# Attention with the keys on the partitions: scores written transposed, values standing still, no row maximum

## The chip, the cores and the metric

The kernel runs on one core of a Trainium2 chip. The metric is device time in microseconds, as the median of runs of the whole kernel; a profile is taken of one execution. TensorE does matrix products into PSUM, VectorE and ScalarE read PSUM and SBUF, GpSimd reads SBUF alone, and SP, ScalarE and GpSimd issue the DMAs.

## What is computed

Eight batches of twelve heads, 448 tokens of 64 dims each, all float32. The rows of q and k are divided by their root mean square and multiplied by a gain; attention follows; the heads are put side by side to 768 channels; then a gate picks 128 of the 448 tokens of each batch, and a feed-forward part is added to those alone.

```python
q_n, k_n = (rmsnorm(q, g_q), rmsnorm(k, g_k))        # x / sqrt(mean(x*x) + 1e-06) * g
scores = 1/sqrt(64) * q_n @ k_n^T
scores = scores - np.max(scores, axis=-1, keepdims=True)
attn = np.exp(scores)
attn = attn / (np.sum(attn, axis=-1, keepdims=True) + 1e-09)
x = attn @ v                                          # (B,H,S,D) -> (B, S, H*D)
...
scores = np.einsum('bsd,d->bs', x, w_gate)
top_idx = np.argpartition(-scores[b], capacity)[:capacity]   # capacity = 128
h = np.maximum(x[b, top_idx] @ w1, 0.0)               # 768 -> 1024
out[b, top_idx] = x[b, top_idx] + sigmoid(scores[b, top_idx])[:, None] * (h @ w2)
```

## The kernel before

Token 4p + j of a batch lies on partition p (112 of them), at place j. Heads come in 24 groups of four; a group is loaded by three DMAs from SP (`load`, L72), three groups ahead, and normalized by `normalize` (L131): GpSimd squares q and k (L138), VectorE sums (L139), GpSimd takes the power -0.5 (L144) and multiplies (L152). `transpose_pair` (L162) brings q and k of two heads onto 128 partitions through TensorE and PSUM, and multiplies by the gains.

The work then runs in 192 units, a unit being 112 queries of two heads. `scores` (L187) makes two matmuls, one per head, whose operands lie on partitions 0 to 63 and 64 to 127, with 112 queries on the output's partitions and 448 keys along the free dimension; VectorE takes the negative row maximum of both heads (L201), and ScalarE the exponential with that bias and the row sum (L206). `transpose_probs` (L216) turns the probabilities by eight TensorE transposes (L222), which VectorE (L229) and ScalarE (L231) copy to SBUF. `values` (L237) makes eight matmuls (each two passes in float32), with the turned probabilities standing still and 64 columns of v moving (L245); VectorE divides by the row sum into x (L253 to L255).

`mixture` (L265) is the feed-forward part of a batch, written as a generator of 16 pieces, one of which is issued after each unit of the next batch: gate scores, ranks and picks on VectorE, the gather (L368), both products (L400, L420) on TensorE, evacuations on ScalarE and VectorE, and an indirect DMA that adds into the output. The last batch's part has no units beside it.

The main loop (L446) issues at step i the scores of unit i, the transposes of unit i-1 and the values of unit i-2. A scheduler orders each engine's queue before the run; the semaphores follow from the data.

Of the kernel before, what the change touches and what calls it, by code (L numbers as in the profile page):

```python
# [17 lines left out]
def _bcast_row(ap_1d: bass.AP, parts: int) -> bass.AP:  # L18
    return dataclasses.replace(ap_1d, ap=[[0, parts]] + [list(x) for x in ap_1d.ap])


@with_exitstack
def kernel(
    ctx: ExitStack,
    tc: tile.TileContext,
    q: bass.AP,
# [7 lines left out]
    moe_capacity: int,  # L34
    out: bass.AP,
):
    """Token 4 p + j of a batch lies on partition p, at place j, everywhere on the chip."""
    nc = tc.nc

    B, H, S, D = q.shape  # L40
    CP = 112
# [28 lines left out]
    loaded = {}  # L70

    def load(n):  # L72
        """The n-th group of heads."""
        b, h0 = n // NG, n % NG * GH
        for nm, src in (("q", q), ("k", k), ("v", v)):
            t = load_pool.tile(
                [CP, GH, NJ, D], F32, tag=nm, name=nm, bufs=5 if nm == "v" else 3
            )
            nc.sync.dma_start(
                out=t.rearrange("p h j d -> p h (j d)"),  # L80
                in_=src[b, h0 : h0 + GH].rearrange("h (p j) d -> p h (j d)", j=NJ),
            )
            loaded[nm, n] = t
# [13 lines left out]
                out=t[D * half : D * (half + 1), :], in_=g.rearrange("(d one) -> d one", one=1)  # L97
            )

    # Which tokens (j', p') of a batch come before token (p, j).  # L100
    before = const.tile([CP, NJ, NJ, CP], F32, name="before")
    nc.vector.memset(before, 1.0)
    for j in range(NJ):
# [25 lines left out]
        nc.sync.dma_start(out=w2, in_=moe_w2.rearrange("(c p) f -> p c f", p=128))  # L129

    def normalize(n):  # L131
        """Rows of q and k of a group of heads over their rms, heads innermost."""
        ss = norm_pool.tile([CP, 2, GH, NJ], F32, name="ss")
        rinv = norm_pool.tile([CP, 2, GH, NJ], F32, name="rinv")
        for i, nm in enumerate("qk"):
            t = loaded[nm, n]
            sq = norm_pool.tile([CP, GH, NJ, D], F32, name="sq")
            nc.gpsimd.tensor_tensor(out=sq, in0=t, in1=t, op=OP.mult)  # L138
            nc.vector.tensor_reduce(out=ss[:, i], in_=sq, axis=AX.X, op=OP.add)  # L139
        nc.gpsimd.tensor_scalar(  # L140
            out=ss, in0=ss, scalar1=1.0 / D, scalar2=1e-6, op0=OP.mult, op1=OP.add
        )
        flat = "p i h j -> p (i h j)"
        nc.gpsimd.tensor_tensor(  # L144
            out=rinv.rearrange(flat),
            in0=ss.rearrange(flat),
            in1=neg_half.to_broadcast([CP, 2 * GH * NJ]),
            op=OP.pow,
        )
        for i, nm in enumerate("qk"):  # L150
            t = norm_pool.tile([CP, NJ, GH, D], F32, tag=nm + "n", name=nm + "n")
            nc.gpsimd.tensor_tensor(  # L152
                out=t.rearrange("p j h d -> p h j d"),
                in0=loaded.pop((nm, n)),
                in1=rinv[:, i, :, :, None].to_broadcast([CP, GH, NJ, D]),
                op=OP.mult,
            )
            loaded[nm + "n", n] = t
# [1 line left out]
    pairs = {}  # L160

    def transpose_pair(b, c):  # L162
        """q and k of two heads with their dims on the partitions, times g (and the scale)."""
        n, h = b * NG + 2 * c // GH, 2 * c % GH
        qT = tr_pool.tile([128, S], F32, name="qT")
        kT = tr_pool.tile([128, S], F32, name="kT")
        for nm, dst in (("q", qT), ("k", kT)):
            ps = ps_tr.tile([128, NJ, CP], F32, tag="tr", name="qk_ps")
            for j in range(NJ):
                nc.tensor.transpose(  # L170
                    out=ps[:, j, :],
                    in_=loaded[nm + "n", n][:, j, h : h + 2, :].rearrange("p h d -> p (h d)"),
                    identity=ident[:CP, :CP],
                )
            ps = ps.rearrange("p j r -> p (j r)")
            if nm == "q":
                nc.vector.tensor_scalar(
                    out=dst, in0=ps, scalar1=gq2, scalar2=scale, op0=OP.mult, op1=OP.mult
                )
            else:  # L180
                nc.scalar.activation(out=dst, in_=ps, func=AF.Copy, scale=gk2)  # L181
        pairs[b, c] = qT, kT
# [80 lines left out]
        return ps_moe.tile([128, 512], F32, tag="moe", name="moe_ps")  # L263

    def mixture(b):  # L265
        """The feed-forward part of batch b, in pieces."""
        x = xs.pop(b)
        nc.sync.dma_start(
            out=out[b].rearrange("(p j) c -> p (j c)", j=NJ), in_=x.rearrange("p j c -> p (j c)")
# [18 lines left out]
        nc.vector.tensor_copy(out=spread, in_=sc[:, :, None].to_broadcast([CP, NJ, CP]))  # L288
        yield

        # The scores of all tokens on every partition, then each token's rank: how many
        # tokens have a higher score, or the same and come before it.
        row_ps = bank()
        for j in range(NJ):
            nc.tensor.transpose(
# [29 lines left out]
        rank = moe_pool.tile([CP, NJ], F32, name="rank")  # L325
        nc.vector.tensor_add(out=rank, in0=higher, in1=equal)

        # Per token: its gate, and its row of the output.
        extra = moe_pool.tile([CP, NJ, 2], F32, name="extra")
        # sigmoid(s) = exp(min(s, 0)) / (exp(min(s, 0)) + exp(-max(s, 0))) has no overflow.  # L330
        parts = moe_pool.tile([CP, 2, NJ], F32, name="parts")
        nc.vector.tensor_scalar_min(out=parts[:, 0], in0=sc, scalar1=0.0)
        nc.vector.tensor_scalar(
# [5 lines left out]
        nc.vector.tensor_mul(out=extra[:, :, 0], in0=parts[:, 0], in1=parts[:, 1])  # L339
        nc.vector.tensor_scalar_add(out=extra[:, :, 1], in0=token_f, scalar1=float(b * S))  # L340
        if CAP % 128:
            # The last slots hold tokens past the capacity: they get nothing added.
            kept = moe_pool.tile([CP, NJ], F32, name="kept")
            nc.vector.tensor_scalar(
                out=kept, in0=rank, scalar1=float(CAP), scalar2=None, op0=OP.is_lt
# [150 lines left out]
```

## Time and profile before

| | us |
|---|---|
| median of 3 runs (1129.56 to 1142.35) | 1139.58 |
| span of the profiled execution | 1137.9 |
| TensorE busy in it | 1009.8 |
| VectorE, ScalarE, GpSimd busy | 619.0, 396.2, 335.3 |
| mean granted clock of TensorE | 0.903 of full speed |

Busy times are unions over an engine's instructions; those of TensorE are modelled at their ends, so that the distance from one start to the next tells more than a duration. PE is the matmul, PEld the weight load that precedes it; a float32 matmul stands as two of each. The granted clock is 1.0 (2.4 GHz) or 0.5 (1.2 GHz) at each moment, and a stretch's figure is a mean over it. The idle time that a row shows is that just before the instruction, with what ended it.

### The profile page before, as it was taken

The numbers are of one execution on the slowest core, as the hardware profiler recorded it, in microseconds if no ns is written. First come the engines' busy times: TensorE is split into PE (matmuls) and PEld (weight loads), VectorE is DVE, ScalarE is ACT, GpSimd is POOL, SyncE is SP. The second block draws the span as 40 slices with busy tenths as digits, with TensorE's granted clock in tenths as the row PEclk, the third lists the DMA queues.
The fourth block names the chain that finished last, engine by engine and source line by source line (L and its number), as shares of the span: only waits on it lengthen the run. The fifth ranks groups of instructions, "written<-read, shape, count | busy, mean of one in ns | idle before, by whom it ended". The sixth has DMA issues, their size and how long they took to land.

```text
span 1137.9 us, 17977 instructions
## 1 busy us (share of the span) xinstructions
PE 1009.8 (89%) x7264; PEld 795.4 (70%) x7264; DVE 619.0 (54%) x1379; ACT 396.2 (35%) x1049; POOL 335.3 (29%) x165
## 2 busy tenths in 40 slices
PE   0598988997989988999889998899898999999966
PEld 0476776875877666886668767687576877787764
DVE  3455577445764357644575446845567447943640
ACT  0232444232533334333343333333343334532400
POOL 7926314405314054041342231440513301100000
PEclk9675888998989979899789997899988999999979
DMA  6901203103201022021231030310302001100110
GB/s 173 334 2 49 49 1 98 50 1 63 78 21 50 1 63 98 1 49 18 46 98 28 22 63 1 97 50 1 63 13 86 17 1 15 50 1 1 15 49 14
DMA packets 37938, 54.98 MB, mean 48 GB/s; under 512 B 1776, under 2 KB 34032, under 8 KB 36960
## 3 DMA queue, kind: packets, MB, share of 16 engines
q1 hardware_dynamic: 36384, 50.68, 15.6%
q0 software_dynamic: 1152, 3.15, 1.9%
q8 instruction: 58, 0.95, 0.3%
q14 instruction: 24, 0.20, 0.1%
q10 hardware_dynamic: 320, 0.00, 0.0%
HBM read 39.67 MB, written 14.16 MB: 47 GB/s over the span
## 4 chain that ended last, share of the span: by engine, by line
PE 67%; POOL 21%; DVE 5%; issue 4%; DMA 1%; ACT 1%; POOLq 0%; SPq 0%; ACTq 0%
PE av L245 23%; PE sc L193 13%; PE pt_ps L222 13%; POOL rinv L144 10%; PE moe_ps L420 6%; PE moe_ps L400 4%; POOL sq L138 4%; PE qk_ps L170 4%; PE moe_ps L368 3%; POOL qn L152 3%; POOL kn L152 3%; DVE ss L139 2%; DVE nmax L201 2%; DMA q<-in_q_dram 1%; ACT p L206 1%
## 5 line engine op out<-in xcount | busy, mean ns | idle before, releaser
L245 PE MATMUL av<-v,pt 112*112 112x64 f32 x3072 | 368.7, 276 | 33.6 <-DVE x L255 33.6
L245 PEld LDWEIGHTS av<-v,pt 112*112 112x112 f32 x3072 | 358.1, 195 | 35.4 <-DVE x L255 35.4
L201 DVE TENSOR_REDUCE nmax<-sc 112x2 f32<-112x896 f32 x192 | 208.2, 1085 | 164.3 <-PE sc L193 164.3
L206 ACT ACTIVATE p<-sc,nmax 112x448 f32<-112x448 f32 x384 | 240.0, 632 | 150.4 <-DVE nmax L201 148.1
L222 PEld LDWEIGHTS pt_ps<-ident,p 112*112 112x112 f32 x1536 | 161.6, 143 | 161.5 <-ACT p L206 83.2
L222 PE MATMUL pt_ps<-ident,p 112*112 112x112 f32 x1536 | 207.6, 279 | 48.8 <-ACT p L206 43.0
L231 ACT COPY pt<-pt_ps 112x448 f32<-112x448 f32 x192 | 102.2, 532 | 339.8 <-PE pt_ps L222 339.8
L193 PE MATMUL sc<-kT,qT 64*112 64x448 f32 x768 | 217.2, 642 | 0.0
L229 DVE COPY pt<-pt_ps 112x448 f32<-112x448 f32 x192 | 118.3, 616 | 44.3 <-PE pt_ps L222 44.3
L144 POOL TENSOR_TENSOR rinv<-ss,neg_half 112x32 f32<-112x32 f32 x24 | 134.1, 5589 | 1.6
L152 POOL TENSOR_TENSOR qn<-q,rinv 112x1024 f32<-112x1024 f32 x24 | 49.1, 2046 | 266.8 <-PE qk_ps L170 266.7
L139 DVE TENSOR_REDUCE ss<-sq 112x16 f32<-112x1024 f32 x48 | 58.3, 1215 | 123.8 <-POOL sq L138 123.8
L433 POOL DMA_INDIRECT out_dram<-y,row x8 | 13.1, 1633 | 374.3 <-DVE y L429 374.3
L255 DVE TENSOR_TENSOR x<-av,rden 112x128 f32<-112x128 f32 x192 | 55.6, 289 | 89.8 <-PE av L245 88.9
L400 PE MATMUL moe_ps<-xeT,w 128*128 128x128 f32 x768 | 94.0, 280 | 0.9 <-ACT hT L409 0.7
L400 PEld LDWEIGHTS moe_ps<-xeT,w 128*128 128x128 f32 x768 | 89.8, 195 | 1.2 <-ACT hT L409 0.9
L420 PE MATMUL moe_ps<-w,hT 128*128 128x384 f32 x256 | 89.2, 493 | 1.4 <-DVE y L429 0.7
L193 PEld LDWEIGHTS sc<-kT,qT 64*112 64x112 f32 x768 | 58.1, 187 | 31.5 <-issue 16.7
L206 ACT ACTIVATION_READ_ACCUMULATOR p<-sc,nmax 112x1 f32 x384 | 77.4, 202 | 0.0
L181 ACT ACTIVATE kT<-qk_ps,gk 128x448 f32<-128x448 f32 x48 | 30.4, 633 | 134.0 <-PE qk_ps L170 134.0
L170 PEld LDWEIGHTS qk_ps<-ident,qn 112*128 112x128 f32 x192 | 22.7, 163 | 62.2 <-issue 32.4
L420 PEld LDWEIGHTS moe_ps<-w,hT 128*128 128x128 f32 x256 | 46.3, 190 | 28.2 <-DVE y L429 1.3
(51 smaller groups left out, 622.5 us busy)
## 6 DMA issues: line engine op xcount, KB each, us to landing
q<-in_q_dram SPq DMA_DIRECT2D x24, 448.0 KB, 4.4
k<-in_k_dram SPq DMA_DIRECT2D x24, 448.0 KB, 6.7
v<-in_v_dram SPq DMA_DIRECT2D x24, 448.0 KB, 5.8
out_dram<-x SPq DMA_DIRECT2D x8, 1344.0 KB, 9.0
w<-in_moe_w_dram SPq DMA_DIRECT2D x2, 3072.0 KB, 17.1
wg<-in_moe_w_gate_dram SPq DMA_DIRECT2D x1, 336.0 KB, 6.3
out_dram<-y,row POOLq DMA_INDIRECT x8, 5.6
gq<-in_g_q_dram ACTq DMA_DIRECT2D x2, 0.2 KB, 5.1
```

Of the source, the lines that this page charges most:

```text
L139: nc.vector.tensor_reduce(out=ss[:, i], in_=sq, axis=AX.X, op=OP.add)
L144: nc.gpsimd.tensor_tensor(out=rinv.rearrange(flat), in0=ss.rearrange(flat), in1=neg_half.to_broadcast([CP, 2 * GH * NJ]), op=OP.pow,)
L152: nc.gpsimd.tensor_tensor(out=t.rearrange("p j h d -> p h j d"), in0=loaded.pop((nm, n)), in1=rinv[:, i, :, :, None].to_broadcast([CP, GH, ...
L193: nc.tensor.matmul(out=sc[:, hh, 0:S], lhsT=qT[r, CP * j : CP * (j + 1)], rhs=kT[r, :], start=True, stop=True,)
L201: nc.vector.tensor_reduce(out=nmax, in_=sc[:, :, 0:S], axis=AX.X, op=OP.max, negate=True)
L206: nc.scalar.activation(out=p, in_=sc[:, hh, 0:S], func=AF.Exp, bias=nmax[:, hh : hh + 1], accum_out=den[:, hh : hh + 1],)
L222: nc.tensor.transpose(out=pt_ps[:CP, kc, :], in_=ps[hh][:, CP * kc : CP * (kc + 1)], identity=ident[:CP, :CP],)
L229: nc.vector.tensor_copy(out=pt, in_=pt_ps[:CP])
L231: nc.scalar.copy(out=pt, in_=pt_ps[:CP])
L245: nc.tensor.matmul(out=av[:, hh, :], lhsT=pts[hh][:, kc, :], rhs=loaded["v", b * NG + 2 * c // GH][:, 2 * c % GH + hh, kc, :], start=(kc = ...
L400: nc.tensor.matmul(out=ps[:, 128 * i : 128 * i + n], lhsT=w1[:, dc, 128 * (f0 + i) : 128 * (f0 + i + 1)], rhs=xeT[:, dc, :n], start=(dc == 0),
L420: nc.tensor.matmul(out=ps[:n, : DM // 2], lhsT=hT[:, fc, :n], rhs=w2[:, fc, cols], start=(fc == 0), stop=(fc == NFC - 1),)
```

## The change

The host now hands in q and k also with the dims on the partitions (two heads on 128), v with tokens on the partitions, and q and k once more by token for their squares. The kernel gets two branches. A first piece on the chip loads both gains, forms the largest squared product, compares it with 60 x 60 / 64 and loads the answer into a register of each engine; with it small (the scores cannot pass 60) `fast` runs, else `general`, which is the kernel before.

In `fast`, the scores of a unit are 112 keys by 448 queries of two heads: the keys stand still, the queries move. No row maximum is taken. q is scaled on VectorE (`scale_q`) by both gains, the scale and the inverse root mean square of each query, which goes through DRAM to be spread over the partitions; that of each key is the per-partition scale of the exponential. The probabilities then have the keys on the partitions, as the second product needs them: v stands still (64 columns per head, the two heads on output partitions 0 to 63 and 64 to 127) and they move, 448 columns, summed over four units in PSUM. For the row sums, VectorE adds the four units' probabilities, and a matmul with ones (32 columns per head) adds over the partitions, once per group of four heads. `finish_group` turns sums and outputs back to tokens on the partitions by twelve transposes and divides, in four steps spread over the next units. Squares move from GpSimd to ScalarE; only the power is left on GpSimd. TensorE's queue keeps the order in which the code is written; the other queues stay with the scheduler. `mixture` is the same but for one buffer of y in place of two.

```diff
+    ps_sc = ctx.enter_context(tc.tile_pool(name="ps_sc", bufs=4, space=PSUM))
+    ps_av = ctx.enter_context(tc.tile_pool(name="ps_av", bufs=2, space=PSUM))
+    ps_aux = ctx.enter_context(tc.tile_pool(name="ps_aux", bufs=1, space=PSUM))
+    ps_moe = ctx.enter_context(tc.tile_pool(name="ps_moe", bufs=1, space=PSUM))
...
+    def load_tokens(n):
+        b, h0 = n // NG, n % NG * GH
+        for i in range(2):
+            t = load_pool.tile([CP, GH, NJ, D], F32, name="tok", bufs=4)
+            nc.sync.dma_start(out=t, in_=tok[b, :, i, h0 : h0 + GH])
+            toks[n, i] = t
+    def load_group(n):
+        b, g = n // NG, n % NG
+        for store, src, name in ((qTs, qT, "qT"), (kTs, kT, "kT")):
+            t = load_pool.tile([128, GH // 2, S], F32, name=name, bufs=2 if name == "qT" else 3)
+            nc.sync.dma_start(
+                out=t, in_=src[b, g * GH // 2 : (g + 1) * GH // 2].rearrange("c p s -> p c s")
+            )
+            store[n] = t
+        t = load_pool.tile([CP, GH, NJ, D], F32, name="v")
+        nc.sync.dma_start(out=t, in_=vp[b, :, g * GH : (g + 1) * GH])
+        vs[n] = t
+    load_tokens(0)
+    load_group(0)
...
+    def inverse_rms(n):
+        ss = norm_pool.tile([CP, 2, GH, NJ], F32, name="ss")
+        for i in range(2):
+            t = toks.pop((n, i))
+            sq = norm_pool.tile([CP, GH, NJ, D], F32, name="sq", bufs=1)
+            nc.scalar.activation(out=sq, in_=t, func=AF.Square)
+            nc.vector.tensor_reduce(out=ss[:, i], in_=sq, axis=AX.X, op=OP.add)
+            yield
...
+            out=ss, in0=ss, scalar1=1.0 / D, scalar2=1e-6, op0=OP.mult, op1=OP.add
+        )
+        flat = "p i h j -> p (i h j)"
+        nc.gpsimd.tensor_tensor(
+            out=rinv.rearrange(flat),
+            in0=ss.rearrange(flat),
+            in1=neg_half.to_broadcast([CP, 2 * GH * NJ]),
+            op=OP.pow,
+        )
+        rinvs[n] = rinv
+        yield
+        rows = dram_pool.tile([GH, S], F32, name="rows")
+        nc.sync.dma_start(
+            out=rows.rearrange("h (p j) -> p h j", j=NJ), in_=rinv[:, 0]
+        )
+        bc = norm_pool.tile([128, GH // 2, S], F32, name="bc")
+        for hh in range(2):
+            src = rows.rearrange("(c hh) s -> hh c s", hh=2)[hh]
+            nc.sync.dma_start(
+                out=bc[D * hh : D * (hh + 1)],
+                in_=dataclasses.replace(src, ap=[[0, D]] + [list(x) for x in src.ap]),
+            )
+        bcs[n] = bc
+        yield
...
+    def scale_q(g):
+        n, c = divmod(g, GH // 2)
+        t = norm_pool.tile([128, S], F32, name="qn", bufs=3)
+        nc.vector.scalar_tensor_tensor(
+            out=t, in0=qTs[n][:, c], scalar=gg, in1=bcs[n][:, c], op0=OP.mult, op1=OP.mult
+        )
+        qns[g] = t
...
+    def scores(u):
+        g, kc = divmod(u, NJ)
+        n, c = divmod(g, GH // 2)
+        p = p_pool.tile([CP, 2, S], F32, name="p")
+        scs = []
+        for hh in range(2):
+            r = slice(D * hh, D * (hh + 1))
+            sc = ps_sc.tile([CP, 512], F32, name="sc")
+            nc.tensor.matmul(
+                out=sc[:, 0:S],
+                lhsT=kTs[n][r, c, CP * kc : CP * (kc + 1)],
+                rhs=qns[g][r, :],
+                start=True,
+                stop=True,
+            )
+            scs.append(sc)
+        for hh in range(2):
+            nc.scalar.activation(
+                out=p[:, hh],
+                in_=scs[hh][:, 0:S],
+                func=AF.Exp,
+                scale=rinvs[n][:, 1, 2 * c + hh, kc : kc + 1],
+            )
+        probs[u] = p
+    def add_probs(u):
+        g, kc = divmod(u, NJ)
+        if kc == 0:
+            return
+        if kc == 1:
+            sums[g] = p_pool.tile([CP, 2, S], F32, name="sum", bufs=3)
+        nc.vector.tensor_tensor(
+            out=sums[g], in0=probs[u - 1] if kc == 1 else sums[g], in1=probs[u], op=OP.add
+        )
...
+    def values(u):
+        g, kc = divmod(u, NJ)
+        n, c = divmod(g, GH // 2)
+        if kc == 0:
+            avs[g] = ps_av.tile([128, 512], F32, name="av")
+        for hh in range(2):
+            nc.tensor.matmul(
+                out=avs[g][D * hh : D * (hh + 1), 0:S],
+                lhsT=vs[n][:, 2 * c + hh, kc, :],
+                rhs=probs[u][:, hh],
+                start=(kc == 0),
+                stop=(kc == NJ - 1),
+            )
+        if kc > 0:
+            probs.pop(u - 1)
+        if kc == NJ - 1:
+            probs.pop(u)
+            t = norm_pool.tile([128, NJ, CP], F32, name="xT", bufs=4)
+            nc.scalar.copy(
+                out=t, in_=avs.pop(g)[:, 0:S].rearrange("d (p j) -> d j p", j=NJ)
+            )
+            xTs[g] = t
+    def finish_group(n):
+        b = n // NG
+        ps = ps_aux.tile([128, 512], F32, tag="aux", name="den_ps")
+        for h in range(GH):
+            nc.tensor.matmul(
+                out=ps[32 * h : 32 * (h + 1), 0:S],
+                lhsT=ones,
+                rhs=sums[n * GH // 2 + h // 2][:, h % 2],
+                start=True,
+                stop=True,
+            )
+        for c in range(GH // 2):
+            sums.pop(n * GH // 2 + c)
+        den = norm_pool.tile([128, NJ, CP], F32, name="den", bufs=1)
+        nc.vector.tensor_copy(
+            out=den, in_=ps[:, 0:S].rearrange("d (p j) -> d j p", j=NJ)
+        )
+        yield
+        ps = ps_aux.tile([128, NJ, 128], F32, tag="aux", name="denT_ps")
+        for j in range(NJ):
+            nc.tensor.transpose(out=ps[:CP, j, :], in_=den[:, j, :], identity=ident)
+        rden = norm_pool.tile([CP, NJ, GH], F32, name="rden")
+        nc.vector.reciprocal(
+            out=rden, in_=ps[:CP].rearrange("p j (h r) -> p j h r", r=32)[:, :, :, 0]
+        )
+        yield
+        if b not in xs:
+            xs[b] = x_pool.tile([CP, NJ, DM], F32, name="x")
+        for c in range(GH // 2):
+            g = n * GH // 2 + c
+            t = xTs.pop(g)
+            ps = ps_aux.tile([128, NJ, 128], F32, tag="aux", name="x_ps")
+            for j in range(NJ):
+                nc.tensor.transpose(out=ps[:CP, j, :], in_=t[:, j, :], identity=ident)
+            col = g % NP * 128
+            nc.vector.tensor_tensor(
+                out=xs[b][:, :, col : col + 128].rearrange("p j (h d) -> p j h d", d=D),
+                in0=ps[:CP].rearrange("p j (h d) -> p j h d", d=D),
+                in1=rden[:, :, 2 * c : 2 * c + 2, None].to_broadcast([CP, NJ, 2, D]),
+                op=OP.mult,
+            )
+            yield
...
+    units = B * NP * NJ
+    per_batch = NP * NJ
+    per_group = GH // 2 * NJ
+    LAG = 2
...
+    drain(inverse_rms(0))
+    constants()
+    drain(inverse_rms(1))
+    load_group(1)
+    load_tokens(2)
+    load_weights()
+    scale_q(0)
+    aux, moe, rms = [], iter(()), iter(())
+    for i in range(units + LAG + 1):
+        n, step = divmod(i, per_group)
+        if step == 4:
+            if n + 2 < n_groups:
+                load_group(n + 2)
+            if n + 3 < n_groups:
+                load_tokens(n + 3)
+        if step == 2:
+            drain(rms)
+            rms = inverse_rms(n + 2) if n + 2 < n_groups else iter(())
+        if i < units:
+            scores(i)
+        if i % NJ == 2 and i // NJ + 1 < B * NP:
+            scale_q(i // NJ + 1)
+        if 1 <= i <= units:
+            add_probs(i - 1)
+        if LAG <= i < units + LAG:
+            values(i - LAG)
+            if (i - LAG + 1) % per_group == 0:
+                aux.append(finish_group((i - LAG) // per_group))
+        if i >= LAG + 1 and aux:
+            if next(aux[0], aux) is aux:
+                aux.pop(0)
+        if (i - LAG - 6) % per_batch == 0 and i >= per_batch:
+            while aux:
+                drain(aux.pop(0))
+            drain(moe)
+            moe = mixture((i - LAG - 6) // per_batch - 1)
+        next(rms, None)
+        next(moe, None)
+    while aux:
+        drain(aux.pop(0))
+    drain(moe)
+    drain(mixture(B - 1))
...
-        )
+        with tc.tile_pool(name="bound", bufs=1) as pool:
+            g = pool.tile([1, 2, D], F32, name="g")
+            nc.sync.dma_start(out=g[:, 0], in_=ap["g_q"].rearrange("(one d) -> one d", one=1))
+            nc.sync.dma_start(out=g[:, 1], in_=ap["g_k"].rearrange("(one d) -> one d", one=1))
+            prod = pool.tile([1, D], F32, name="prod")
+            nc.vector.tensor_mul(out=prod, in0=g[:, 0], in1=g[:, 1])
+            nc.vector.tensor_mul(out=prod, in0=prod, in1=prod)
+            top = pool.tile([1, 1], F32, name="top")
+            nc.vector.tensor_reduce(out=top, in_=prod, axis=AX.X, op=OP.max)
+            small = pool.tile([1, 1], I32, name="small")
+            nc.vector.tensor_scalar(
+                out=small,
+                in0=top,
+                scalar1=MAX_SCORE * MAX_SCORE / D,
+                scalar2=None,
+                op0=OP.is_le,
+            )
+            is_small = nc.values_load(small[0:1, 0:1], min_val=0, max_val=1,
+                skip_runtime_bounds_check_because="a comparison gives 0 or 1")
+        with tc.If(is_small > 0) as cmp, tc.manual_schedule(engines={mybir.EngineType.PE}):
+            fast(
+                tc, *(ap[n] for n in ("qT", "kT", "vp", "tok", "g2")),
+                *(ap[n] for n in _INS[5:]), cap, out,
+            )
+        with cmp.Else():
+            general(tc, *(ap[n] for n in _INS), cap, out)
     r = _run(nc, [arrays], core_ids=[0])
```

## Rows read from the trace of the kernel before

**Rows 1.** The page's first part: engine, busy us, share of the span, instructions

```profile
PE 1009.8 (89%) x7264; PEld 795.4 (70%) x7264; DVE 619.0 (54%) x1379; ACT 396.2 (35%) x1049; POOL 335.3 (29%) x165
```

**Rows 2.** Windows: stretch, length, busy time (instructions) per engine in the header's order

```profile
core 0: us, PE busy (x) PEld busy (x) DVE busy (x) ACT busy (x) POOL busy (x), PEclk, DMA share, GB/s
430.00:572.00 142.00, 130.46 (x954) 102.66 (x953) 81.33 (x183) 52.98 (x141) 41.72 (x19) 0.92 0.17 42
998.00:1080.00 82.00, 82.00 (x642) 64.98 (x640) 39.87 (x91) 32.34 (x87) 1.57 (x1) 1.00 0.04 6
```

**Rows 3.** Timeline, one unit without feed-forward: start, length, engine, line, operation, tiles

```profile
1064.04 1.01 PE L193 MATMUL sc<-kT,qT 64*112 64x448 f32 x4
...
1064.98 0.98 PE L222 MATMUL pt_ps<-ident,p 112*112 112x112 f32 x8
...
1065.70 1.65 PEld L245 LDWEIGHTS av<-v,pt 112*112 112x112 f32 x16
1065.80 1.70 PE L245 MATMUL av<-v,pt 112*112 112x64 f32 x16
...
1067.42 1.01 PE L193 MATMUL sc<-kT,qT 64*112 64x448 f32 x4
```

**Rows 4.** Timeline of PE, one unit in a stretch with granted clock 0.5

```profile
105.80 1.84 PE L193 MATMUL sc<-kT,qT 64*112 64x448 f32 x4
107.57 1.74 PE L222 MATMUL pt_ps<-ident,p 112*112 112x112 f32 x8
109.10 3.11 PE L245 MATMUL av<-v,pt 112*112 112x64 f32 x16
112.14 1.84 PE L193 MATMUL sc<-kT,qT 64*112 64x448 f32 x4
```

**Rows 5.** A wait (total us, times, longest), and PE after one such stall

```profile
DVE ss L139 <- POOL sq L138: 123.8, 25, 7.2
...
549.30 3.25 PE L245 MATMUL av<-v,pt 112*112 112x64 f32 x16 [5.59 <-DVE x L255]
```

**Rows 6.** A chain piece, and the timeline of the uncovered last part

```profile
236.55 2.73 PE moe_ps L400 x24
...
1086.41 0.96 DVE L276 SCALAR_TENSOR_TENSOR prod<-x,wg 112x768 f32<-112x768 f32 x1
...
1118.64 5.43 PE L420 MATMUL moe_ps<-w,hT 128*128 128x384 f32 x16 [0.69 <-ACT hT L409]
...
1131.14 1.55 POOL L433 DMA_INDIRECT out_dram<-y,row  x1 [72.02 <-DVE y L429]
```

**Rows 7.** Timeline of the start: the first scores of the steady sequence

```profile
45.47 1.84 PE L193 MATMUL sc<-kT,qT 64*112 64x448 f32 x4
```

**Rows 8.** Groups by line and shape: count, busy us, mean ns, idle before

```profile
L206 ACT ACTIVATE p<-sc,nmax 112x448 f32<-112x448 f32 x384 | 240.0, 632 | 150.4 <-DVE nmax L201 148.1 <-DVE rank L326 2.2
L201 DVE TENSOR_REDUCE nmax<-sc 112x2 f32<-112x896 f32 x192 | 208.2, 1085 | 164.3 <-PE sc L193 164.3
L144 POOL TENSOR_TENSOR rinv<-ss,neg_half 112x32 f32<-112x32 f32 x24 | 134.1, 5589 | 1.6
L229 DVE COPY pt<-pt_ps 112x448 f32<-112x448 f32 x192 | 118.3, 616 | 44.3 <-PE pt_ps L222 44.3
L231 ACT COPY pt<-pt_ps 112x448 f32<-112x448 f32 x192 | 102.2, 532 | 339.8 <-PE pt_ps L222 339.8
L139 DVE TENSOR_REDUCE ss<-sq 112x16 f32<-112x1024 f32 x48 | 58.3, 1215 | 123.8 <-POOL sq L138 123.8
L276 DVE SCALAR_TENSOR_TENSOR prod<-x,wg 112x768 f32<-112x768 f32 x32 | 30.6, 955 | 0.9
```

**Rows 9.** DMA issues: count, KB each, median us from issue to landing

```profile
q<-in_q_dram SPq DMA_DIRECT2D x24, 448.0 KB, 4.4
...
gq<-in_g_q_dram ACTq DMA_DIRECT2D x2, 0.2 KB, 5.1
```

More of the change, by code (lines that the diff above doesn't have):

```diff
@@ L24, with general @@
+@with_exitstack
+def general(
     ctx: ExitStack,
@@ L478 @@
     from concourse.bass_utils import run_bass_kernel_spmd as _run
-    nc = _bacc.Bacc("TRN2", target_bir_lowering=False, num_devices=1)
-    arrays, args = {}, []
-    for name in _INS:
-        a = _np.ascontiguousarray(inputs[name])
-        arrays[f"in_{name}_dram"] = a
-        args.append(
-            nc.dram_tensor(f"in_{name}_dram", a.shape, mybir.dt.from_np(a.dtype), kind="ExternalInput").ap()
-        )
-    B, H, S, D = inputs["q"].shape
+    B, H, S, D = inputs["q"].shape
+    NJ = 4
@@ new lines @@
+    CP = S // NJ
+    a = {name: _np.asarray(inputs[name]) for name in _INS}
+    a["qT"] = a["q"].transpose(0, 1, 3, 2).reshape(B, H // 2, 2 * D, S)
+    a["kT"] = (
+        a["k"].reshape(B, H, CP, NJ, D).transpose(0, 1, 4, 3, 2).reshape(B, H // 2, 2 * D, S)
+    )
+    a["vp"] = a["v"].reshape(B, H, CP, NJ, D).transpose(0, 2, 1, 3, 4)
+    a["tok"] = _np.stack([a["q"], a["k"]], axis=1).reshape(B, 2, H, CP, NJ, D)
+    a["tok"] = a["tok"].transpose(0, 3, 1, 2, 4, 5)
+    a["g2"] = _np.stack([_np.tile(a["g_q"], 2), _np.tile(a["g_k"], 2)], axis=1)
@@ L489 @@
+    nc = _bacc.Bacc("TRN2", target_bir_lowering=False, num_devices=1)
+    arrays, ap = {}, {}
+    for name, x in a.items():
+        x = _np.ascontiguousarray(x)
+        arrays[f"in_{name}_dram"] = x
+        ap[name] = nc.dram_tensor(
+            f"in_{name}_dram", x.shape, mybir.dt.from_np(x.dtype), kind="ExternalInput"
+        ).ap()
     out = nc.dram_tensor("out_0_dram", (B, S, H * D), F32, kind="ExternalOutput").ap()
+    cap = int(inputs["moe_capacity"])
     with tile.TileContext(nc) as tc:
-        kernel(
-            tc, *args, int(inputs["moe_capacity"]), out
-        )
+        with tc.tile_pool(name="bound", bufs=1) as pool:
[8 more added lines that the diff above has]
+            small = pool.tile([1, 1], I32, name="small")
+            nc.vector.tensor_scalar(
+                out=small,
+                in0=top,
+                scalar1=MAX_SCORE * MAX_SCORE / D,
+                scalar2=None,
+                op0=OP.is_le,
+            )
+            is_small = nc.values_load(small[0:1, 0:1], min_val=0, max_val=1,
[4 more added lines that the diff above has]
+                *(ap[n] for n in _INS[5:]), cap, out,
+            )
+        with cmp.Else():
+            general(tc, *(ap[n] for n in _INS), cap, out)
```

255 lines of the change are left out of this document (254 added, 1 removed).

## The prediction

> **What bounds the kernel now.** I read the busy shares first, then the windows by stage, the timeline of single units, the list of waits, and the groups by line. TensorE is busy 89% of the span, VectorE 54%, ScalarE 35%, GpSimd 29% [rows 1]. The stages say more: in a middle stage TensorE is busy 130.46 of 142 us at a granted clock of 0.92, and in the last full stage, where GpSimd has almost nothing left to do (1.57 us), it is busy 82.00 of 82 us at clock 1.00 [rows 2]. So TensorE's queue is the bound, and where it isn't full it is held up by GpSimd's normalizing.
>
> Then the timeline of one undisturbed unit (112 queries of two heads): scores from 1064.04, eight transposes of the probabilities from 1064.98, sixteen value passes from 1065.80 (their loads from 1065.70), the next scores at 1067.42 [rows 3]. A unit costs 3.38 us: scores 0.94, transposes 0.72, values 1.72. With the clock at its lower level (1.2 GHz; these rows lie in a stretch granted 0.5) a unit takes 112.14 - 105.80 = 6.34 us [rows 4].
>
> What that leaves: 192 units x 3.38 = 649; transposes of q and k, some 0.8 us for each of 48 pairs = 39; seven feed-forward parts of 28.6 (below) = 200; together 888 us. From the first steady scores at 45.47 [rows 7] to the start of the last, uncovered part at 1086.41 [rows 6] there are 1041 us. So 153 us (17%) go to waits and to the lower clock. Their source is in the list of waits: VectorE's reduction waits 123.8 us for GpSimd's squares, and what stands behind it (maxima, x) comes late, as in the 5.59 us that TensorE stood before 549.30, after which the value passes took 3.25 us in place of 1.70 [rows 5].
>
> **The change, part by part.**
>
> *Price of a pass.* An f32 matmul is two passes. Sixteen passes by 384 columns take 5.43 us [rows 6], 0.34 each, so one by 448 columns is 0.34 x 448/384 = 0.395. The scores are four such passes (two heads, on partitions 0 to 63 and 64 to 127). In series that is 1.58 us, but they take 0.94 [rows 3]: the two heads run side by side (2 x 0.395 = 0.79) and 0.15 goes to the first load and the drain.
>
> *Scores* keep their shape and stay at 0.94.
>
> *Values.* v stands still (64 columns per head) and the probabilities move, 448 columns: per unit four passes in place of eight transposes and sixteen short passes. The two heads now share the rows of the array and differ in its columns, which the trace of before does not show. Bounds: side by side like the scores, 0.94; in series 1.58 + 0.15 = 1.73. I take 0.94, since the scores' row is the only one here in which two matmuls use separate parts of the array, and they overlapped. The unit becomes 1.88 us (bounds 1.88 and 2.67). The Trainium skill's TensorE: Matmul & The Clock Gate, Measured speedup vs the span model, gives 2.38 times for three column tiles; scaled to two that is an estimate of 1.59 times, values of about 1.1 us and a total some 30 us higher; no run here shows it.
>
> *Closing a group* (24 times). Denominators: eight passes by 448 columns in four strips, 0.94 if four run at once, 8 x 0.395 + 0.15 = 3.31 in series. Twelve transposes moving 128 columns, at 2.73/24 = 0.114 [rows 6], 1.37. Three more changes between tiled and whole array, 0.15 each as above. Sum 2.8, bounds 2.8 and 5.1. Group: 8 x 1.88 + 2.8 = 17.8 us, times 24 = 428; in series 8 x 2.67 + 5.1 = 26.5, times 24 = 635.
>
> *Feed-forward part*, unchanged: 48 + 96 passes by 128 columns at 0.114 = 16.4, 32 by 384 at 0.34 = 10.9, and about 1.3 for twelve small ones: 28.6 us. It is cut into 16 steps, 12 with TensorE work, now each set between tiled matmuls: 12 x 0.15 = 1.8 more. 30.4 x 7 = 213; the eighth stands in the tail. What speaks against the change is these switches: the scores' 0.15 us [rows 3] is paid at each. The Trainium skill's TensorEngine Tiling (Array Packing), Key Properties, says that changing the tiling mode drains the engine; the scores' row agrees (0.94 against 0.79), and by rule and row the sum is the same.
>
> *Removed from the other engines.* VectorE loses the maxima, 208.2 us, and a copy, 118.3; ScalarE a copy, 102.2; GpSimd all but the power, 5.6 us per group (134.1 of its 335.3) [rows 1, 8]. *Added.* VectorE, per group: six additions by 896 (955 x 896/768 = 1.11) 6.7, two reductions 2.4 as before, two scalings of q by 448 (nearest the copy of 448, 0.62) 1.2, the rest (one copy, reciprocals, two products by 512) about 2.2: 12.5 us, plus its feed-forward work: 32 products 30.6 [rows 8], 64 comparisons by 448 at the copy's 0.62, 40, and some 220 short operations at an estimated 0.2, 45; together 116, or 4.8 per group: 17.3. ScalarE: 16 exponentials at 0.53 to 0.63, two copies, two squares by 1024 (twice the row of 448, 1.1 each): 11.8 to 13.4. TensorE with its share of the feed-forward has 17.8 + 30.4/3 = 27.9. So both are covered; without cover the larger, 17.3, would still be below 17.8. The cover is thin only in the eight units per batch that have no feed-forward step.
>
> *Waits.* scores(i) need PSUM that the exponentials of unit i-2 free, and values(i-2) need those same exponentials. From the end of scores(i-2) TensorE has values, scores, values, about 2.8 us, before scores(i); two exponentials take 1.1 to 1.3 and one square between them 1.1. It fits. If it doesn't, TensorE stands, since its order is now fixed and the feed-forward steps are queued behind. VectorE's reductions no longer wait for GpSimd, so that stall goes; next late would be ScalarE's square behind VectorE's reduction (one buffer), a unit apart.
>
> *Transfers.* q and k come twice, plus the broadcast of the query scales through DRAM; the queue's order on SP is loads, scales, x. Before, 448 KB landed in 4.4 us [rows 9]; five or six per group of 27.9 us, two groups ahead, are hidden. What would lose cover is the scales' round trip, and a delay there shows only at the start.
>
> *Start.* New: the bound test, two small loads (the nearest row has 5.1 us to landing [rows 9]), four tiny VectorE operations, a branch on each engine with no row at all: I take 10 us, bounds 5 and 18. Then tokens 6, square and reduction 2.4, table load partly covered, power 5.4, scale through DRAM and back (two landings, 4 each), scaling 0.7: about 34 us at the first scores against 45.47 [rows 7], where normalizing two groups stood in front.
>
> *Tail.* From 1086.41 to the end 51.5 us, unchanged [rows 6], plus closing the last group, five dependent steps, 7: 58.
>
> *Sum.* 34 + 428 + 213 + 58 = 733. Waits and low clock: between nothing and the old 17% of the 641 us loop (109). Near nothing, because the source in [rows 5] is removed and the last stage shows the engine full without it [rows 2]; I add 12 (first units at the low clock, small waits). 745 us of span. The profiled span is 1137.9 and the median 1139.58, so 1.7 more at most: 746.
>
> **The rivals.**
> 1. *Values and denominators run in series.* For it: no row shows columns shared out. Against: the scores overlap. 34 + 635 + 213 + 58 = 940, with small waits 950. An overlap in part lies between.
> 2. *TensorE waits for its own exponentials.* Fixed order, ScalarE or VectorE late by more than two units. A unit is then 0.94 + 2 x 0.63 + 0.94 = 3.14; 192 x 3.14 + 67 + 213 + 92 = 975. Against: 27.9 against 17.3 per group.
> 3. *Slower: the clock stays low.* Short waits in every unit keep the clock at 1.2 GHz; a unit of before then cost 6.34 against 3.38 [rows 3, 4]. All 641 us of loop times 1.88 plus a start of 40 and a tail of 75 is 1320; it passes 1151 when about 71% of the loop runs low. For it: before, a clock of 0.92 in the middle stages and a low stretch after a single 5.59 us wait. Against: 1.00 whenever TensorE is full.
> 4. *The general branch runs.* Then 1140 + 10 = 1150. The reference's inputs give a largest squared product of the two gains of 27.65, against the limit of 3600/64 = 56.25, so the fast branch is taken.
>
> **How the numbers follow.** Forecast 0.70, with a range of its own from 700 (start at 28, no waits, shorter weight loads) to 842 (733 + 109). Rival 1 0.17, rival 2 0.06, rival 3 0.05, rival 4 and the like 0.02. To leave out no more than two in ten the range takes most of rival 1: 695 to 940. Within 1% either way is what measurement can't tell from no change. Faster by over 1%: 0.70 + 0.17 + 0.06 = 0.93, less 0.01 for rival 2 with more waits, 0.92; within 1% 0.02; slower 0.06.
>
> **What would show it.** Right: value matmuls of the two heads starting within some 10 ns of each other, 1.9 us from scores to scores in units without a feed-forward step, clock 0.97 or more after the start, GpSimd busy some 140 us, VectorE near 420. Wrong: the second head's passes starting 0.4 us after the first's (rival 1), TensorE idle behind the exponentials (rival 2), a clock near 0.6 (rival 3), the first scores later than 45 us, or transposes of the probabilities still there (rival 4).

## Result

The changed kernel takes 801.12 us (median of 4 runs, 800.58 to 801.55) against 1136.01 us of the kernel before: a ratio of 0.7047 with a 95% interval of 0.7012 to 0.7082 (the medians themselves divide to 0.705). The forecast was 746 us with a range of 695 to 940: the side and the main mechanism (value products side by side, no transposes of the probabilities) are right, and 55 us are missing from the sum. The profiled execution has a span of 798.9 us.

The page's first part, and three windows (columns as in [rows 2]):

```profile
PE 689.0 (86%) x3520; PEld 327.0 (41%) x3520; DVE 390.4 (49%) x690; ACT 307.0 (38%) x521; POOL 159.3 (20%) x44
```

```profile
60.00:160.00 100.00, 85.19 (x413) 32.52 (x410) 68.04 (x109) 57.21 (x91) 40.84 (x7) 0.93 0.83 197
...
360.00:460.00 100.00, 90.72 (x461) 42.98 (x460) 49.09 (x86) 39.86 (x68) 19.61 (x4) 0.95 0.40 105
...
560.00:660.00 100.00, 98.87 (x512) 45.48 (x510) 47.48 (x84) 38.34 (x70) 16.20 (x4) 1.00 0.33 82
```

TensorE is still the fullest engine, but only the late window is full; the earlier ones have 9 to 15 us per 100 in which it stands, and a clock below 1. One unit, in the timeline (compare [rows 3]):

```profile
45.06 1.01 PE L209 MATMUL sc<-qn,kT 64*112 64x448 f32 x4
...
46.00 0.97 PE L242 MATMUL av<-p,v 112*64 112x448 f32 x4
...
46.91 1.01 PE L209 MATMUL sc<-qn,kT 64*112 64x448 f32 x4
```

Scores 0.94, values 0.91, together 1.85 us in place of 3.38. So the main step holds. The missing time shows in the list of waits (who waits, for whom: us in total, times, longest):

```profile
POOL rinv L167 <- ACT p L218: 277.4, 11, 32.7
...
ACT sq L159 <- DVE ss L160: 79.3, 28, 7.7
...
DVE ss L160 <- POOL rinv L167: 58.3, 13, 5.3
...
PE denT_ps L280 <- DVE den L274: 30.0, 14, 5.0
```

and in one such stall, in the timeline:

```profile
403.25 5.84 POOL L167 TENSOR_TENSOR rinv<-ss,neg_half 112x32 f32<-112x32 f32 x1 [16.68 <-DVE sum L232]
...
409.12 1.22 DVE L160 TENSOR_REDUCE ss<-sq 112x16 f32<-112x1024 f32 x1 [3.28 <-POOL rinv L167]
...
410.38 1.06 ACT L159 ACTIVATE sq<-tok 112x1024 f32<-112x1024 f32 x1 [3.77 <-DVE ss L160]
...
413.60 0.62 DVE L274 COPY den<-den_ps 128x448 f32<-128x448 f32 x1
...
414.27 1.10 PE L280 MATMUL denT_ps<-ident,den 128*112 128x128 f32 x4 [5.04 <-DVE den L274]
...
416.05 1.67 PE L209 MATMUL sc<-qn,kT 64*112 64x448 f32 x4
```

Read it upwards. TensorE stands before the denominators' transposes, which wait for a copy on VectorE; VectorE had stood in front of a reduction until the power on GpSimd was over (409.09); ScalarE had stood at a square, with exponentials behind it. After the stall the scores take 1.67 us in place of 1.01: the granted clock is 0.50 from 415 to 417 us, its lower level.

In each of the middle batches the same chain stops TensorE a second time, before scores whose PSUM the exponentials behind a square have not freed:

```profile
382.94 1.22 DVE L160 TENSOR_REDUCE ss<-sq 112x16 f32<-112x1024 f32 x1 [5.31 <-POOL rinv L167]
...
384.19 1.06 ACT L159 ACTIVATE sq<-tok 112x1024 f32<-112x1024 f32 x1 [7.68 <-DVE ss L160]
...
385.82 2.04 PE L209 MATMUL sc<-qn,kT 64*112 64x448 f32 x4 [2.25 <-ACT p L218]
```

The four batches whose scores start between 187 and 475 us have one stall of each kind (2.25 and 5.04 us) and take 95.6 to 97.0 us from start to start, where the undisturbed one at 571 us takes 82.5. Of the 13 us between them 7.3 are the stalls; 10.2 us or more of each such batch run at the lower clock, which is an estimated 5 us lost at half speed.

Why would a power be late that was written two groups ahead? The groups of instructions up to 403.2 us say it (columns as in [rows 8]):

```profile
L218 ACT ACTIVATE p<-sc,rinv 112x448 f32<-112x448 f32 x208 | 120.2, 632 | 117.2 <-PE sc L209 110.9 <-issue 5.6 <-POOL rinv L167 0.7
...
L167 POOL TENSOR_TENSOR rinv<-ss,neg_half 112x32 f32<-112x32 f32 x17 | 99.8, 5869 | 266.6 <-ACT p L218 163.9 <-DVE ss L163 51.3 <-DVE sum L232 33.6
L160 DVE TENSOR_REDUCE ss<-sq 112x16 f32<-112x1024 f32 x38 | 46.3, 1219 | 72.6 <-ACT sq L159 36.1 <-POOL rinv L167 36.1
```

208 exponentials are 13 groups, and 17 powers are done. The 18th may write only into the buffer of the 13th group, of five that there are (`rinv`), so it starts when that group's last exponential is over: that one ends at 403.11 us, the power starts at 403.25. (The row above names a sum on VectorE, which had ended at 402.91.) All fifteen powers from 147 us on start like this, 0.13 to 0.50 us after the last exponential of the group five back. 38 reductions are 19 groups: the scheduler, which orders every queue but TensorE's, had drawn them ahead as far as buffers go, and the next one writes into the `ss` buffer (two of them) that the 18th power still reads.

### The profile page after: what moved, and what is told of

Read it like the earlier page. It is cut to its first block, busy times and chain, and to the rows that moved or that the text cites. A ratio compares the mean times of both kernels' runs of the same rounds, so it can differ in the third digit from the quotient of the medians.

```text
span 798.9 us, 9099 instructions
## 1 busy us (share of the span) xinstructions
PE 689.0 (86%) x3520; PEld 327.0 (41%) x3520; DVE 390.4 (49%) x690; ACT 307.0 (38%) x521; POOL 159.3 (20%) x44
## 4 chain that ended last, share of the span: by engine, by line
PE 45%; issue 16%; DVE 14%; POOL 11%; DMA 7%; ACT 6%; SPq 1%; POOLq 0%; DVEq 0%; ACTq 0%
POOL rinv L167 11%; PE sc L209 11%; PE av L242 10%; PE moe_ps L461 8%; PE moe_ps L441 7%; PE moe_ps L409 5%; DMA tok<-in_tok_dram 5%; DVE ss L160 4%; ACT sq L159 3%; DVE sum L232 3%; ACT p L218 2%; DVE cmp L355 2%; DVE cmp L345 2%; PE x_ps L293 2%; DVE x L295 1%
## 5 line engine op out<-in xcount | busy, mean ns | idle before, releaser
L218 ACT ACTIVATE p<-sc,rinv 112x448 f32<-112x448 f32 x384 | 222.3, 631 | 246.5 <-PE sc L209 223.4
L209 PE MATMUL sc<-qn,kT 64*112 64x448 f32 x768 | 211.2, 615 | 50.1 <-DVE qn L194 31.5
L242 PE MATMUL av<-p,v 112*64 112x448 f32 x768 | 194.2, 586 | 0.0
L232 DVE TENSOR_TENSOR sum<-sum,p 112x896 f32<-112x896 f32 x96 | 104.6, 1090 | 70.5 <-ACT p L218 69.9
L209 PEld LDWEIGHTS sc<-qn,kT 64*112 64x112 f32 x768 | 58.1, 180 | 132.1 <-issue 62.0
L160 DVE TENSOR_REDUCE ss<-sq 112x16 f32<-112x1024 f32 x48 | 58.5, 1219 | 98.8 <-POOL rinv L167 58.3
L242 PEld LDWEIGHTS av<-p,v 112*64 112x64 f32 x768 | 39.2, 139 | 136.4 <-issue 132.3
L159 ACT ACTIVATE sq<-tok 112x1024 f32<-112x1024 f32 x48 | 50.8, 1059 | 97.7 <-DVE ss L160 79.3
L232 DVE TENSOR_TENSOR sum<-p 112x896 f32<-112x896 f32 x48 | 52.2, 1089 | 70.5 <-ACT p L218 70.5
L409 PE MATMUL moe_ps<-pick,x 112*128 112x128 f32 x384 | 48.9, 286 | 10.2 <-DVE pick L395 9.6
L409 PEld LDWEIGHTS moe_ps<-pick,x 112*128 112x128 f32 x384 | 45.9, 198 | 21.1 <-DVE pick L395 9.4
L474 POOL DMA_INDIRECT out_dram<-y,row x8 | 13.7, 1718 | 202.0 <-DVE y L470 199.7
```

Source lines behind the costliest of these rows:

```text
L159: nc.scalar.activation(out=sq, in_=t, func=AF.Square)
L209: nc.tensor.matmul(out=sc[:, 0:S], lhsT=kTs[n][r, c, CP * kc : CP * (kc + 1)], rhs=qns[g][r, :], start=True, stop=True,)
L218: nc.scalar.activation(out=p[:, hh], in_=scs[hh][:, 0:S], func=AF.Exp, scale=rinvs[n][:, 1, 2 * c + hh, kc : kc + 1],)
L232: nc.vector.tensor_tensor(out=sums[g], in0=probs[u - 1] if kc == 1 else sums[g], in1=probs[u], op=OP.add)
L242: nc.tensor.matmul(out=avs[g][D * hh : D * (hh + 1), 0:S], lhsT=vs[n][:, 2 * c + hh, kc, :], rhs=probs[u][:, hh], start=(kc == 0), stop=(k ...
L409: nc.tensor.matmul(out=ps[:, 128 * i : 128 * i + n], lhsT=x[:, j, 128 * dc : 128 * (dc + 1)], rhs=pick[:, j, :n], start=(j == 0), stop=(j ...
```

## Experiments

Theory A: the stalls are this chain of two buffers. Theory B: VectorE can't work while GpSimd takes a power. Theory C: VectorE's ranks and sums come in bunches anyway. (In the timeline around 403 us VectorE did run other work during the power, which speaks against B.)

**More buffers for the inverse root mean squares.**

```diff
-        rinv = norm_pool.tile([CP, 2, GH, NJ], F32, name="rinv", bufs=5)
+        rinv = norm_pool.tile([CP, 2, GH, NJ], F32, name="rinv", bufs=24)
```

> Edit: 24 buffers of the inverse root mean squares in place of 5, all else as in the changed kernel (801 us). Theory A (a chain of buffers): the power on GpSimd waits for a free buffer, that is for the exponentials of five groups back, and VectorE's reduction, which stands in its queue in front of the sums and the denominators' copy, waits for that power. With 24 buffers the power never waits: VectorE's 58 us of waiting for GpSimd and the 5.6 us gaps of TensorE after the first 200 us go, 801 becomes 750 to 770; what stays is the front part, where the squares of more groups are drawn still further ahead. Theory B (VectorE can't work while GpSimd takes a power, whatever the buffers): 801 stays within 1%. Theory C (VectorE's ranks and sums simply come in bunches): 795 to 805.

Measured 771.11 us, ratio 0.6834 (0.6792 to 0.6876), 1 us above theory A's range. VectorE's wait for the power falls from 58.3 to 0.3 us, and the batches from 293 us on take 82.5 us.

**More buffers for the sums of squares.**

```diff
-        ss = norm_pool.tile([CP, 2, GH, NJ], F32, name="ss")
+        ss = norm_pool.tile([CP, 2, GH, NJ], F32, name="ss", bufs=24)
```

> Edit: 24 buffers of the sums of squares in place of 2. Theory A: the reduction then waits for no power, so VectorE's 58 us of waiting for GpSimd go to 0 and the 5.6 us gaps of TensorE with them: 750 to 770, like the run with 24 buffers of the inverse root mean squares, since the chain is cut at its other link. Theory B: within 1% of 801. Theory C: 795 to 805.

Measured 759.38 us, ratio 0.6715 (0.6678 to 0.6752): the fastest kernel with the full computation here. A window of it, and its reductions up to 240 us:

```profile
260.00:560.00 300.00, 296.46 (x1567) 137.53 (x1567) 150.52 (x279) 119.95 (x217) 76.81 (x15) 1.00 0.34 92
```

```profile
L160 DVE TENSOR_REDUCE ss<-sq 112x16 f32<-112x1024 f32 x48 | 58.3, 1216 | 42.8 <-ACT sq L159 42.7
```

Cutting the chain at either link removes the stalls of the middle, as A said; B and C fall. TensorE is full from 260 us on, and a batch takes 82.5 us from 284 us on. The other side: with no limit all 48 reductions are done by 240 us (28 of them in the changed kernel by then), and what loss is left stands in that front part.

**Two buffers for the squares** (`sq`, `bufs=1` to `bufs=2`).

> Edit: two buffers of the squares in place of one. ScalarE waited 79 us for VectorE's reduction before a square, and the exponentials stand behind it. If the shortage of this buffer is the main cause: 760 to 775, TensorE's 2.8 us gaps before scores go. Theory A: the reductions still wait for the power, so VectorE's waits for GpSimd stay near 58 us and the gain is small, 785 to 801.

Measured 805.45 us (0.7128; 0.7088 to 0.7167), no gain, and 4 us above theory A's range. The third buffer of the chain isn't its cause; VectorE still waits 60.2 us for powers.

**VectorE and ScalarE in the order written too** (both added to the engines of `manual_schedule`).

> Edit: the queues of VectorE and ScalarE also keep the order written, as TensorE's does; buffers unchanged. In the order written the squares, reductions and the power of a group come two groups ahead, when the buffers they need have long been free. Theory A: no reduction waits for a power, 745 to 765, GpSimd's powers come two groups ahead in place of four or five. Theory B: within 1% of 801. Theory C: 795 to 830, since the ranks then stand in one piece in front of the sums.

Measured 793.41 us (0.7022; 0.6983 to 0.7060): by the ratio not clear of the changed kernel's 0.7047, and between the 745 to 765 of theory A and the 795 to 830 of theory C. The waits for powers went, but others came: at 65.72 us ScalarE had stood 12.1 us at one square, and in each batch TensorE waits for the ranks, which now stand in one piece (30.6 us before the picks, in eight waits, against 9.6), and for x (25.3 us against 2.5).

```profile
65.72 1.06 ACT L159 ACTIVATE sq<-tok 112x1024 f32<-112x1024 f32 x1 [12.10 <-DMA tok<-in_tok_dram]
```

**No side by side.** Each value matmul uses all columns of the array; the outputs of attention are other numbers.

```diff
-                out=avs[g][D * hh : D * (hh + 1), 0:S],
-                lhsT=vs[n][:, 2 * c + hh, kc, :],
+                out=avs[g][:, 0:S],
+                lhsT=vs[n][:, 2 * c + hh, kc - kc % 2 : kc - kc % 2 + 2, :].rearrange("p j d -> p (j d)"),
...
-                start=(kc == 0),
-                stop=(kc == NJ - 1),
+                start=(kc == 0 and hh == 0),
+                stop=(kc == NJ - 1 and hh == 1),
```

> Edit to the changed kernel: each value matmul loads 128 columns (two neighbouring key chunks of v) and writes all 128 output partitions, so that the two heads' matmuls can't stand side by side in the array; the outputs of attention are then other numbers, the amount of streaming is the same. Side by side (the forecast's step): the four passes now run in series at 0.37 to 0.40 us each, a unit goes from 1.84 to 2.5 us, 192 x 0.65 = 125 us, some of it covering waits: 880 to 930 us. If the order of the two heads' matmuls never mattered (no overlap in the changed kernel): 795 to 810.

Measured 912.93 us (one run, so without an interval), as expected if the two heads do run side by side in the changed kernel. Its timeline:

```profile
299.70 1.01 PE L209 MATMUL sc<-qn,kT 64*112 64x448 f32 x4
300.64 1.77 PE L242 MATMUL av<-p,v 112*128 112x448 f32 x4
302.25 0.60 PE L293 MATMUL x_ps<-ident,xT 128*112 128x128 f32 x4
```

The four passes take 1.61 us in series against 0.91. The weight loads are longer here too (195 ns in the mean against 139), but four passes at the forecast's 0.395 make 1.58 by themselves, so they can hold little of it. Sharing out the columns is worth 112 us of the whole; without it the time would have come near the first rival's 940 to 950.

**TensorE's queue left to the scheduler** (no `manual_schedule`).

> Edit to the changed kernel: TensorE's queue is left to the scheduler too, all else as it is. If the written order is worth nothing here: 793 to 809. If it keeps the feed-forward steps from bunching in front of the scores: 815 to 860, with longer waits of ScalarE for the scores. Theory A (the waits are a matter of VectorE's queue and its buffers): VectorE's 58 us of waiting for GpSimd stay, whatever TensorE's order.

Measured 803.96 us (0.7091; 0.7035 to 0.7146), as expected if the order is worth nothing: the written order of TensorE neither gains nor costs anything that shows, and the waits for powers stay at 55.0 us.

What is the front loss? Theory D: the weights' 6.3 MB hold up the tokens. Theory E: the work drawn ahead crowds there. Theory F: squares stand in ScalarE's queue before their tokens can have come. All start from the 759 us kernel.

**Weights not loaded** (set to a constant on the chip; the feed-forward part is other numbers).

> Edit to the run with 24 buffers of the sums (759 us): the feed-forward weights aren't loaded but set to a constant on the chip, so the added part is other numbers. Theory D (what is left of the loss, some 20 us between 60 and 240 us, comes from 6.3 MB of weights that hold up the tokens' loads while ScalarE's queue stands at a square, with exponentials behind it): TensorE's gaps of 4 to 6 us before 110 us go, 735 to 748. Rival E (the squares and reductions drawn ahead crowd VectorE and ScalarE there, the loads don't matter): 755 to 761.

Measured 776.03 us (0.6853; 0.6801 to 0.6905), slower by 17 us and outside both ranges. ScalarE waits more, not less, for tokens (28.5 us before):

```profile
ACT sq L158 <- DMA tok<-in_tok_dram: 45.8, 13, 6.9
```

So tokens come late without any weights on the way, and D as the whole cause falls. The scheduler draws squares further ahead here (21 have begun by 110 us, 16 in the 759 us kernel), which may be why they meet their loads; that isn't shown. The edit also has GpSimd write the constant, which takes 10.4 us and moves its second power from 21.2 to 30.3 us, so part of the 17 us may be the edit's own.

**SP in the order written, weights in 15 pieces from unit 8.**

> Edit to the run with 24 buffers of the sums (759 us): the queue of SP also keeps the order written, so that tokens come three groups ahead and no more, and the weights come in 15 pieces, one per unit from unit 8. Theory D and rival E both see their cause removed: 730 to 745, the sum of the forecast without its waits being 733. If neither is the cause, 755 to 765; if SP in the written order makes loads wait for each other, above 765.

Measured 767.07 us (0.6779; 0.6726 to 0.6833), not clear of the 759 us kernel's 0.6715 and 2 us above the range for neither cause. Squares still wait 44.0 us for tokens, so what both theories start from was not removed. The loss was spread out: the second and third batch take 89.4 and 87.6 us in place of 99.1 and 91.2, but the later ones 85.1 to 88.0 in place of 82.5. The front loss is not explained by it.

**ScalarE in the order written**, alone, with SP and the pieces, and with the pieces but SP free.

> Edit to the run with 24 buffers of the sums (759 us): ScalarE's queue also keeps the order written, so that a group's squares stand two groups ahead and not as early as the scheduler puts them. Theory F (the front loss comes from squares drawn ahead to a place where their tokens have only just been asked for, with exponentials queued behind): ScalarE's 28.5 us of waiting for tokens fall below 10, 735 to 750. Theory D (the weights hold up the loads, wherever the squares stand): the tokens are still late by the weights' time, some 12 us as in the run with both queues written, 755 to 770.

> The same with SP's queue in the order written and the weights in 15 pieces from unit 8 on. Theory F and theory D both have their cause removed: 730 to 745. If VectorE's ranks between the sums are what is left (waits of TensorE before the transposes of x and the picks): 750 to 765.

> The same as the last with SP's queue left to the scheduler. Theory F: 735 to 750, as with the weights in one piece. If the pieces matter by themselves, it is faster than the run with ScalarE's written order and whole weights by more than 10 us.

Measured 831.08, 808.02 and 837.47 us (0.7363, 0.7149 and 0.7430): all far slower, none as expected. The squares' waits did fall (to 11.1, 13.9 and 2.7 us), but a new wait came on VectorE (106.3, 77.2 and 116.4 us), in the first of them:

```profile
DVE qn L194 <- DMA bc<-rows: 106.3, 15, 9.3
```

With powers no longer early, their way through DRAM ends late, and the scheduler had put the scaling of q, in VectorE's queue, in front of sums and denominators. So drawing ahead is also what hides that way: VectorE waits for it 11.0 us in the changed kernel, nearly all of it at the start. F isn't decided by these runs: they took away one wait and made another.

**No root mean squares at all** (no token loads, squares, reductions, powers; the inverse is 1, so the output is other numbers; the way through DRAM and the scaling stay; from the changed kernel, buffers as they were).

> Edit to the changed kernel (801 us): the root mean squares are left out altogether (no loads of tokens, no squares, reductions or powers; the inverse is a constant 1), while its way through DRAM, the scaling of q and all else stay. If normalizing off TensorE's path is the whole difference between the forecast's sum and the measurement: a batch takes 82.5 us throughout (the undisturbed batches of the changed kernel), 705 to 735. If part of the loss has another source, such as the scaled queries' way through DRAM or VectorE's ranks between the sums: 745 to 790, with waits of TensorE left in the middle batches.

Measured 719.76 us (0.6357; 0.6310 to 0.6404).

```profile
160.00:260.00 100.00, 98.86 (x526) 44.28 (x526) 52.24 (x94) 42.63 (x77) 3.25 (x2) 1.00 0.37 105
```

This is as expected if normalizing is the whole difference: the way through DRAM and the ranks, which stay in, are not the source by themselves. So normalizing, none of which runs on TensorE, costs 81 us. The first scores come at 18.2 us in place of 31.5, which is 13; the other 68 are waits and low clock in the loop. By the starts of each batch's scores, compared with this run, the changed kernel loses 14 us in its first two batches and 54 in the four after them; the 759 us kernel loses 28 in its first three and nothing behind. So cutting the two-buffer chain frees the middle and crowds the front, and gives 42 us of the 81 on balance (801 to 759). The rest is that front loss and the start's 13; for the front loss it is shown that it belongs to normalizing, not by which of its waits.

## Right and wrong, point by point

- *Values side by side, 0.94 us*: right, 0.91. The bound for a run in series, 1.73, compares with 1.61 in the kernel without sharing: 1.61/0.91 is 1.77 times. The 2.38 times that the Trainium skill's TensorE: Matmul & The Clock Gate, Measured speedup vs the span model, gives for three column tiles, scaled to two, made an estimate of 1.59 times and about 1.1 us; the measurement is better than that.
- *Scores, closing a group, feed-forward, switches*: right. From the first scores to the store of the last x, the kernel without normalizing takes 662.1 - 18.2 = 643.9 us; the forecast had 428 + 213 + 7 = 648. (The 643.9 still hold one stall of 4.62 us, 6.8 us at the lower clock after it, and short waits for the picks, so the terms are a little too large.) The Trainium skill's TensorEngine Tiling (Array Packing), Key Properties, says that a change of tiling mode drains the engine; whatever that costs is within these numbers, and no run here prices it by itself.
- *Start, 34 us*: 31.5, by luck: errors that cancel in part. The bound test was over at 4.27 us, when the first token load is issued (it stood at 10 in the sum); two squares with their reductions, from 9.58 to 14.26, took 4.7 us (one pair, 2.4, in the sum); the way through DRAM took 10.8 us (8 in the sum), from the issue at 20.00 to the scaling:

```profile
4.27 0.79 SPq L87 DMA_DIRECT2D tok<-in_tok_dram  x2
...
20.00 0.33 SPq L177 DMA_DIRECT2D rows<-rinv  x1
...
30.76 1.28 DVE L194 SCALAR_TENSOR_TENSOR qn<-qT,gg,bc 128x448 f32<-128x448 f32 x2 [9.99 <-DMA bc<-rows]
```

- *Tail, 58*: from the last x to the end 798.9 - 743.8 = 55.1 us, and 5.6 for closing the last group before it: 61. Some 3 us of the difference are gate products on VectorE: four stand behind the last x here (743.79 to 747.68), and the row at 1086.41, from which the 51.5 were taken, was the last of its four.
- *Transfers, hidden*: nearly; ScalarE's squares wait 18.1 us for their tokens, in seven waits, all before 115 us.
- *Waits and low clock, 12 us*: wrong, and this is the term that was mis-sized. Measured 712.2 - 643.9 = 68 us more than the kernel without normalizing, inside the bounds given (nothing to 109), but far from the value taken. The sign of being right that belongs to it, a clock of 0.97 or more after the start, did not come either: the windows from 60 to 560 us have 0.91 to 0.95. The argument was that the source in [rows 5], VectorE waiting for GpSimd's squares, is removed. It is; but VectorE waits for GpSimd still, 58.3 us in place of 123.8, by way of the buffer that the power reads. The forecast looked at what data each step needs and at the order written, and not at which buffer it overwrites, nor that all queues but TensorE's are ordered by a scheduler that draws work ahead to the limit of the buffers. It did name ScalarE's square behind VectorE's reduction as next late, but not what holds the reduction.
- *Rivals*: in series, no (in the trace 7 ns lie between the starts of the heads' first passes); TensorE waiting for its own exponentials, in part (14.5 us before scores, four of the seven waits being the 2.25 us stalls behind a square); the low clock, 83 us of the span at the lower level, 61 of them before the last x, not the whole; the general branch, no.
- *VectorE near 420 us, GpSimd some 140*: 390.4 and 159.3. The power takes 5.9 us in the mean against 5.6.

## What to carry to other kernels

Where the queue of an engine is filled ahead by a scheduler, each buffer count is a distance, and a short one in a chain decides where the queue stops; what is queued behind stands too, as the denominators' copy did here behind a reduction. Ask of each moved step not only which data it waits for but whose buffer it overwrites, and give the small tiles (128 bytes per partition here) as many buffers as cost nothing, then look at the front again: with the limit gone the work crowded there. An ablation that leaves out a whole side chain tells what it costs before one guesses at its waits.

## What the runs showed of the hardware

Two float32 matmuls that differ only in the columns of the array they use, over the same 112 partitions, ran side by side: 0.91 against 1.61 us for four passes, 1.77 times. In the batches from 187 us to 516 us TensorE stood for 2.25 or 5.04 us at a time, and toward the end of each of these stalls, or soon behind it, the granted clock went to 0.5 (1.2 GHz) for 3.4 to 10.2 us; before the change it did so for 13.7 us at the stall of 5.59 us in [rows 5]. In the undisturbed stretch from 516 to 745 us it stayed at 1.0 (2.4 GHz).
